# Moving seven buffers of a Fourier-and-attention kernel by 128 bytes, onto multiples of 256

## The chip, the cores and the metric

The kernel runs on one core of a Trainium2 chip. The metric is the device time of one execution in microseconds; the figure given is the median of several runs.

## What is computed

The input x has 2048 rows (the sequence) and 576 columns. A gate mixes linear attention (32 heads of 18 columns) with the real part of a two-dimensional Fourier transform, done as matrix products with given cosine and sine matrices. All data is float32.

```
qkv = x @ wqkv;  phi(t) = where(t > 0, t + 1, exp(t)) + 1e-6
kv  = einsum("bhsd,bhse->bhde", phi(k), v);  z = phi(k) summed over s
o   = einsum("bhqd,bhde->bhqe", phi(q), kv) / (phi(q) . z + 1e-6)
a   = o @ wo
y   = seq_re @ (x @ hid_re.T) - seq_im @ (x @ hid_im.T)
out = g * a + (1 - g) * y,   g = sigmoid((x * gate_w).sum(-1))
```

## The kernel before

**Precision.** Each float32 operand is split into a high part, rounded by ScalarE as it copies (`hi_of`, L175), and a low part, the rest, by VectorE (`lo_of`, L185). A product is three matmuls: high by high, high by low, low by high. Every matmul takes 128 columns of weights (the operand that stays in the array, 512 bytes a partition) and nearly always moves 288 columns past them (half of 576, 1152 bytes a partition). The result goes to one of eight banks.

**Stages, in order.** The K projection (L532, then `run` at L205); the V accumulation, which forms phi(k) times x (L696) and from it the kv matrices (L678, L681); the Q projection (L205, weights `wq`), with the products of kv and wo between; transposes and the output projection (L205, `mw` and `qs`); then, once for the real and once for the imaginary matrices, the hidden transform (L979) and the sequence transform (L1133).

**The two transforms** use a scheme with seven products in place of eight for a two-by-two block matrix: sums and differences of quarters are formed on VectorE (`add`, L195), split into high and low, and multiplied. In `Hidden.run` the order of products is written out by hand: eight passes p over rows of x, in each seven products k, of seven matmuls each (L979), the weights of the array being parts of x (`xf`, `xb`, `xr`) and the moving operand the transform's matrix (`wf`). Its results become the factors `fh` (high) and `fl` (low). In `sequence` 32 batches n follow, each with a piece of the sequence matrix (`craw` as it lands, `c` once split). A batch has seven products of two times three matmuls, 42 in all (L1133): `c` is the weights, `fh` and `fl` the moving operand.

**Buffers.** All tiles lie in one array per partition, the arena, at offsets that are written out by hand. At its start are eight pieces (T_AT) that hold first phi(k) and later the factors, then an accumulator (ACC_AT), then seven slots of 7168 bytes, then small buffers (Y_AT, where the ring `es` of tiles `e` lies, and CONST_AT). Four slots take `craw` and the low parts of `c`, three the high parts; the first batch of each transform lies in the first region, so 62 of the 64 batches are in slots. Between uses the slots hold parts of other stages: tiles of x and the weights `wq` in the K and Q projections, and parts of `xf`, `xb`, `xr` and `wf` in the hidden transforms. The lines that set this:

```
T_AT = 0
ACC_AT = T_AT + NP * TPAIR
SLOT_AT, SLOT = ACC_AT + NT * D * 4 + 256, 7 * BS * P * 4     # L70
Y_AT = SLOT_AT + 7 * SLOT + 512                               # L71
LAY_Q = dict(xs=(-256, 4864, 9984, 43776), hi=(15104, 20864), lo=(26688, 31296))
WF_AT = MIX_AT + 4 * D * 4
WF = 5 * HALF * 4
base = (nc.sbuf_base + 63) // 64 * 64        # every tile lies at base + offset
```

NP is 8, NT 16, D 576, P 128, BS 2, HALF 288, TPAIR 16128 bytes.

`Layout.w(k)` says where the seven `wf` matrices of a hidden transform lie: in the first transform those of k = 3, 4, 5 in slots, in the second those of k = 4, 5, 6, the others beside the accumulator. In the Q projection the four tiles of x lie at the offsets `xs` of LAY_Q (the one at 43776 is replaced by a place in the first region for the Q part), and the weights at `hi` and `lo`, all counted from SLOT_AT.

**What sets the order.** SyncE issues the loads of the sequence matrices (L1070) up to three batches ahead; the orders of TensorE in the later stages, VectorE, ScalarE and SyncE are those in which the program is written. GpSimd issues the stores and loads of the intermediate forms.

Of the kernel before, what the change touches and what calls it, by code (L numbers as in the profile page):

```python
# [14 lines left out]
P = 128  # L15
S, D, H, DH = 2048, 576, 32, 18
NT = S // P
# [8 lines left out]
BS = 2  # L26
# [40 lines left out]
XD = 2 * D * 4  # L67
T_AT = 0
ACC_AT = T_AT + NP * TPAIR
SLOT_AT, SLOT = ACC_AT + NT * D * 4 + 256, 7 * BS * P * 4  # L70
Y_AT = SLOT_AT + 7 * SLOT + 512  # L71
CONST_AT = Y_AT + 2 * D * 4
XS = 10 * P * 4
WH, WL = 5 * HALF * 4, 4 * HALF * 4
# [59 lines left out]
def kernel(  # L134
# [23 lines left out]
    def at(offset, shape, dtype=F, name="t"):  # L158
        count[0] += 1
        t = nc.alloc_sbuf_tensor_at(f"{name}_{count[0]}", list(shape), dtype,  # L160
                                    offset=base + offset)
        return t.ap()
# [200 lines left out]

    es = Ring(Y_AT, 1184, 3)

# [214 lines left out]
    cs_ring = Ring(C_AT, 2 * CU * P * 4, 4)  # L580
    cs_ring.at.append(Y_AT)
    xg_order = [(c, q) for c in range(5) for q in range(NCU)]
# [329 lines left out]
    factors, backlog = [], []  # L912
    y_ring = Ring(Y_AT, HALF * 4, 4)

# [178 lines left out]
    def sequence(m, g, src, dst, last=None, between=None):  # L1093
        late, held, stores, rest_lows = [], [], [], []
        for n in range(NP * NB):
# [45 lines left out]
            if b < NB - 1:  # L1141
                continue
            y = at(Y_AT, [P, 2, 2, HALF], F, "ys")
            c11, c12, c21, c22 = (y[:, i // 2, i % 2] for i in range(4))
# [211 lines left out]
```

## Time and profile before

| | |
|---|---|
| median of 3 runs | 724.93 us (724.75 to 724.96) |
| the profiled execution | 725.31 us, its span 723.6 us |
| TensorE busy | 718.9 us, 5436 matmuls |
| VectorE, ScalarE, GpSimd busy | 594.6, 331.8, 54.1 us |
| moved by DMA | 157.83 MB, mean 218 GB/s |
| granted TensorE clock | 1.000 |

The profile is of one execution. Busy time of an engine is the union of its instructions; matmuls overlap one another, since each is recorded from its start to its modelled end (about 294 ns), while the next starts some 130 ns after it. What a matmul costs is thus the distance from its start to the next one's, not its recorded length.

### The profile page before, as it was taken

To read this page: it belongs to the slowest core of one execution; us is meant where nothing else is said; L and a number is where in the kernel's file an instruction comes from. 1 tells how busy PE (TensorE), PEld (TensorE's weight loads), DVE (VectorE), ACT (ScalarE), POOL (GpSimd) and SP (SyncE) were. 2 spreads that over 40 slices of the span, in tenths; PEclk is the share of its full clock that TensorE was granted. 3 is DMA by queue.
4 is the path that set the end of the run, shared out by engine and by line. 5 is a ranking of instruction groups with operands and counts; after the bars stand their busy time and mean duration, and the time that the engine had idled before them with its cause. 6 is when DMAs were issued, how large, how long until landed. Compare 5 with 4: busy or idle time off the path is not lost.

```text
span 723.6 us, 13786 instructions
## 1 busy us (share of the span) xinstructions
PE 718.9 (99%) x5436; PEld 718.3 (99%) x5436; DVE 594.6 (82%) x954; ACT 331.8 (46%) x519; POOL 54.1 (7%) x94
## 2 busy tenths in 40 slices
PE   9999999999999999999999999999999999999998
PEld 9999999999999999999999999999999999999997
DVE  5699876787999828989999999857889988778884
ACT  5998445678644534453434334223535432342331
POOL 1112200050131100000010000000000000000000
PEclk9999999999999999999999999999999999999999
DMA  7388887874594699544475586889963543454440
GB/s 256 105 286 297 305 304 214 295 223 118 182 358 177 228 321 388 160 153 131 157 249 189 167 289 198 287 313 401 380 214 130 175 143 136 125 179 153 153 154 34
DMA packets 54836, 157.83 MB, mean 218 GB/s; under 512 B 6388, under 2 KB 12084, under 8 KB 53748
## 3 DMA queue, kind: packets, MB, share of 16 engines
q1 hardware_dynamic: 45716, 118.44, 48.5%
q0 software_dynamic: 8768, 38.12, 14.5%
q8 instruction: 43, 0.70, 0.4%
q10 hardware_dynamic: 288, 0.39, 0.2%
q14 instruction: 21, 0.17, 0.1%
HBM read 114.06 MB, written 41.39 MB: 215 GB/s over the span
## 4 chain that ended last, share of the span: by engine, by line
PE 93%; DVE 6%; issue 0%; ACT 0%; DVEq 0%; POOL 0%; POOLq 0%
PE bank L1133 49%; PE bank L205 18%; PE bank L979 14%; PE bank L696 8%; PE bank L532 2%; DVE qs L185 1%; DVE acc L775 1%; DVE pz L767 1%; DVE den L768 1%; PE bank L231 1%; PE bank L678 0%; DVE xb L185 0%; DVE den L772 0%; PE bank L797 0%; DVE xb L195 0%
## 5 line engine op out<-in xcount | busy, mean ns | idle before, releaser
L1133 PE MATMUL bank<-fh,c 128*128 128x288 f32 x1792 | 354.7, 294 | 0.0
L1133 PEld LDWEIGHTS bank<-fh,c 128*128 128x128 f32 x1792 | 286.7, 188 | 0.0
L1133 PE MATMUL bank<-fl,c 128*128 128x288 f32 x896 | 263.6, 294 | 0.0
L175 ACT ACTIVATE c<-craw 128x1792 fp32r<-128x1792 f32 (+1 forms) x84 | 121.3, 1447 | 169.9 <-DVE craw L195 161.2
L1133 PEld LDWEIGHTS bank<-fl,c 128*128 128x128 f32 x896 | 168.7, 188 | 0.0
L185 DVE TENSOR_TENSOR c<-craw,c 128x1792 fp32r<-128x1792 f32 (+4 forms) x86 | 141.9, 1653 | 1.5 <-ACT c L175 1.4
L195 DVE TENSOR_TENSOR craw<-craw 128x256 f32<-128x256 f32 (+1 forms) x192 | 97.9, 512 | 22.0 <-DMA craw<-in_ci_dram 13.6
L205 PE MATMUL bank<-wd,xs 128*128 128x288 f32 (+1 forms) x784 | 105.9, 295 | 0.0
L205 PEld LDWEIGHTS bank<-wd,xs 128*128 128x128 f32 x784 | 104.6, 188 | 0.0
L979 PE MATMUL bank<-wf,xf 128*128 128x288 f32 x588 | 91.1, 295 | 0.0
L979 PEld LDWEIGHTS bank<-wf,xf 128*128 128x128 f32 x588 | 83.4, 189 | 0.0
L205 PE MATMUL bank<-mw,qs 128*128 128x288 f32 x448 | 61.8, 296 | 0.1
L696 PE MATMUL bank<-pk,c 128*128 128x288 f32 x448 | 60.6, 296 | 0.0
L205 PEld LDWEIGHTS bank<-mw,qs 128*128 128x128 f32 x448 | 59.8, 188 | 0.5 <-DVE qs L185 0.4
L696 PEld LDWEIGHTS bank<-pk,c 128*128 128x128 f32 x448 | 59.7, 189 | 0.0
L370 DVE SCALAR_TENSOR_TENSOR acc<-bank,e 128x288 f32<-128x288 f32 x64 | 28.5, 452 | 17.3 <-ACT e L369 17.1
L195 DVE TENSOR_TENSOR ys<-bank,ys 128x288 f32<-128x288 f32 x63 | 28.8, 456 | 16.0 <-PE bank L1133 12.6
L185 DVE TENSOR_TENSOR fl<-fl,fh 128x864 fp32r<-128x864 f32 (+1 forms) x32 | 34.5, 1093 | 6.6 <-ACT fh L175 5.3
L175 ACT ACTIVATE fh<-fl 128x864 fp32r<-128x864 f32 (+1 forms) x32 | 29.8, 950 | 16.6 <-DVE fl L195 16.6
L195 DVE TENSOR_TENSOR fl<-bank,y 128x288 f32<-128x288 f32 x48 | 21.6, 450 | 15.8 <-PE bank L979 15.8
L979 PE MATMUL bank<-wf,xr 96*128 96x288 f32 x112 | 33.3, 298 | 0.0
L195 DVE TENSOR_TENSOR ys<-ys,bank 128x288 f32<-128x288 f32 x47 | 21.2, 450 | 12.4 <-PE bank L1133 11.8
(106 smaller groups left out, 639.6 us busy)
## 6 DMA issues: line engine op xcount, KB each, us to landing
xf<-xm SPq DMA_DIRECT2D x42, 512.0 KB, 8.4
craw<-in_cr_dram SPq DMA_DIRECT2D x32, 512.0 KB, 3.6
craw<-in_ci_dram SPq DMA_DIRECT2D x32, 512.0 KB, 3.7
xm<-xb POOLq DMA_DIRECT2D x8, 1024.0 KB, 5.8
wf<-wm SPq DMA_DIRECT2D x14, 576.0 KB, 6.2
xraw<-in_xa_dram SPq DMA_DIRECT2D x25, 320.0 KB, 3.5
xr<-xr SPq DMA_DIRECT2D x14, 448.0 KB, 8.0
xm<-xb POOLq DMA_DIRECT2D x8, 768.0 KB, 7.4
```

Of the source, the lines that this page charges most:

```text
L175: return nc.scalar.activation(dst, src, AF.Copy, bias=bias)
L185: nc.vector.tensor_tensor(out=dst, in0=src, in1=hi, op=ALU.subtract)
L195: nc.vector.tensor_tensor(out=dst, in0=a, in1=b, op=op)
L205: nc.tensor.matmul(ps, a, b, start=(n == 0), stop=(n == len(pairs) - 1))
L231: nc.tensor.matmul(warm[:, :P], ones_f, ones_f, start=True, stop=True)
L370: nc.vector.scalar_tensor_tensor(dst, ps, 0.0, e, op0=ALU.max, op1=ALU.add)
L532: nc.tensor.matmul(ps[i][h], x[:, i_x * P:(i_x + 1) * P], wkt.row(h, j), start=(c == 0 and n == 0), stop=(c == KC and n == 1))
L696: nc.tensor.matmul(ps[h][:, :HALF], t[:, a, k], pk[s][:, b, half(h)], start=(s == 0 and n == 0), stop=(s == NT - 1 and n == len(passes) - 1))
L767: nc.vector.scalar_tensor_tensor(pz, acc[2 * k + i], EPS, zb, op0=ALU.add, op1=ALU.mult)
L768: nc.vector.tensor_reduce(out=d[:, i], in_=pz.rearrange("p (h d) -> p h d", d=DH), op=ALU.add, axis=AX.X)
L979: nc.tensor.matmul(ps, a, b, start=(start and n == 0), stop=(n == len(ops) - 1), skip_group_check=True)
L1133: nc.tensor.matmul(ps[q], c[x][:, l, k], factors[p](y, f), start=(p == 0 and i == 0), stop=(p == NP - 1 and i == 2))
```

## The change

The start of the slots moves up by 128 bytes, and the gap behind the slots shrinks by as much, so that Y_AT and all behind it stay. In the built program the arena's base is at byte 1152, which is 128 past a multiple of 256; the slots began 128 past such a multiple and begin on one now. No instruction is added, removed or moved on any engine; 289 tiles change their address by 128 bytes: the `c` and `craw` in slots (186 of them), and `xf`, `xs`, `xraw`, `xb`, `wf`, `wd`, `wraw`, `xr`, three tiles of wo and one constant for the warm-up.

```diff
-SLOT_AT, SLOT = ACC_AT + NT * D * 4 + 256, 7 * BS * P * 4
-Y_AT = SLOT_AT + 7 * SLOT + 512
+SLOT_AT, SLOT = ACC_AT + NT * D * 4 + 384, 7 * BS * P * 4
+Y_AT = SLOT_AT + 7 * SLOT + 384
```

## The prediction

> **What bounds the kernel now.** I read the page's engine line first, then who waited for whom on TensorE, then the chain of work that ended last, and last the timeline of single products.
>
> ```profile
> PE 718.9 (99%) x5436; PEld 718.3 (99%) x5436; DVE 594.6 (82%) x954; ACT 331.8 (46%) x519; POOL 54.1 (7%) x94
> ...
> PE bank L231 <- POOL ones_f L224: 1.1, 1, 1.1
> PEld bank L205 <- DVE qs L185: 0.4, 1, 0.4
> ```
>
> The first row is the page: TensorE is busy for 718.9 of 723.6 us. The other two are all the waits that TensorE has in the whole run, with its weight loads: 1.1 us for the first memset and 0.4 us once in the output projection. No transfer is waited for by TensorE anywhere. So the time is a count of matmuls multiplied by the distance between their starts (the pace), and the chain shows the pace by stage:
>
> ```profile
> 20.42 44.59 PE bank L205 x336
> 65.01 19.18 PE bank L696 x144
> 85.16 12.85 PE bank L696 x96
> ...
> 261.68 51.98 PE bank L979 x392
> 313.66 177.16 PE bank L1133 x1344
> 490.82 52.07 PE bank L979 x392
> 542.89 174.03 PE bank L1133 x1320
> ```
>
> Columns: start, length, line, number of matmuls. Length over number gives 132.7 ns for the K projection (L205), 133.2 and 133.9 for the V accumulation (L696), 132.6 and 132.8 for the hidden products (L979), and 131.8 in both sequence stages (L1133). All are 288 columns wide, with weights of 128 columns, at the same granted clock:
>
> ```profile
> 262.00:314.00 52.00, 52.00 (x394) 52.00 (x393) 41.10 (x80) 22.25 (x39) 1.86 (x3) 1.00 0.75 266
> 314.00:491.00 177.00, 177.00 (x1345) 177.00 (x1344) 155.44 (x214) 63.94 (x46) 6.42 (x9) 1.00 0.65 220
> 491.00:543.00 52.00, 52.00 (x394) 52.00 (x392) 42.93 (x83) 21.78 (x38) 0.00 (x0) 1.00 0.89 330
> ```
>
> The last three numbers of a row are granted clock, DMA share and GB/s. The clock is 1.00 in all three stages, and the DMA share goes from 0.65 to 0.89 with the pace moving by 1 ns: the pace does not follow the transfers. What is left to explain 131.8 against 133.9 is the order of the operands and where they lie. That is all this change touches.
>
> **What the addresses are.** In the built program the arena starts at byte 1152 of a partition, 128 past a multiple of 256. T_AT, ACC_AT, the old SLOT_AT and a slot's size are multiples of 256 within it, and weights of 128 columns are 512 bytes. So every full set of weights that lies in a slot now starts 128 past a multiple of 256, and will start on one. Moving operands are 1152 bytes, 4.5 times 256, so neighbours alternate between the two places. No instruction, tile size, buffer reuse or wait changes.
>
> **Part by part.** The sum is made against the profiled execution's own 725.31 us (span 723.6, 1.71 around it); the median of the three runs, 724.93, is 0.38 below it.
>
> *Sequence products (L1133).* 62 of the 64 batches lie in slots, so 62 x 42 = 2604 matmuls get weights that start 128 bytes higher; their moving factors stay. No row shows this stage with weights on a multiple of 256. The nearest row is the stage itself: its batches go round through different slots in the two runs, and both come to 131.8. Whether the weight load could be the limit is seen in the kv-by-wo products before the output projection:
>
> ```profile
> 145.04 1.75 PE L205 MATMUL bank<-plain,kvb 126*126 126x288 f32 x12
> 146.64 3.89 PE L205 MATMUL bank<-wd,xs 128*128 128x288 f32 x28
> 150.37 1.74 PE L205 MATMUL bank<-plain,kvb 126*126 126x288 f32 x12
> 151.94 3.90 PE L205 MATMUL bank<-wd,xs 128*128 128x288 f32 x28
> 155.68 0.95 PE L205 MATMUL bank<-plain,kvb 72*72 72x288 f32 x6
> 156.47 0.70 PE L205 MATMUL bank<-wd,xs 128*128 128x288 f32 x4
> ```
>
> Start to start, the 126-column weights run at 1.60/12 = 133 and 1.57/12 = 131 ns; they begin at all sorts of offsets, since a row of kvb is 126 wide. The 72-column weights, little more than half as much to load, run at 0.79/6 = 132. A load that is almost halved and one at any offset make no pace of their own. I take 0 for this part. The bounds: the fastest six in the next fence run at 130.0 ns, 1.8 below, which is -4.7 us for 2604; L696's slowest row, 133.9, is 2.1 above, +5.5 us.
>
> *Hidden products (L979).* Three of the seven weight matrices of each run lie in slots, and here they are the moving operand; they shift against the other four.
>
> ```profile
> 262.45 0.96 PE L979 MATMUL bank<-wf,xb 128*128 128x288 f32 x6
> 263.25 0.30 PE L979 MATMUL bank<-wf,xr 96*128 96x288 f32 x1
> 263.38 0.95 PE L979 MATMUL bank<-wf,xb 128*128 128x288 f32 x6
> 264.17 0.30 PE L979 MATMUL bank<-wf,xr 96*128 96x288 f32 x1
> 264.31 0.95 PE L979 MATMUL bank<-wf,xb 128*128 128x288 f32 x6
> 265.09 0.30 PE L979 MATMUL bank<-wf,xr 96*128 96x288 f32 x1
> 265.23 0.96 PE L979 MATMUL bank<-wf,xb 128*128 128x288 f32 x6
> 266.03 0.30 PE L979 MATMUL bank<-wf,xr 96*128 96x288 f32 x1
> 266.17 0.95 PE L979 MATMUL bank<-wf,xb 128*128 128x288 f32 x6
> ```
>
> These are products k = 1 to 4 and the start of k = 5. A product is seven matmuls. Their blocks of weights are 5760 bytes, 22.5 times 256, so the high parts start on a multiple of 256 for k = 1 and 4 and 128 past one for k = 2 and 3. From start to start the products take 0.93 and 0.94 us on the multiple, 0.93 and 0.92 off it: 0.01 us more on it, which is as small as the rows can show. (The six of k = 3 take 265.09 - 264.31 = 0.78, 130.0 each.) In the first run two blocks go onto a multiple and one leaves it, in the second all three go onto one: four products more per pass, eight passes, 32 x 0.01 = **+0.3 us**. Bounds 0 and, if each rounding goes against it, +0.6.
>
> By the Trainium skill (SBUF — State Buffer, Who interferes with whom) TensorE reads moving operand and weights through two ports of its own and never waits for another engine; taken strictly, both parts would be 0 and the two rivals on pace below would fall. The rows agree as to the other engines, and differ a little on places, by 0.01 us a product, so I keep those rivals.
>
> *Projections.* In the K projection 336 matmuls get moved weights under unmoved moving operands; the row is 132.7 ns, and the output is as for L1133: 0. In the Q projection all 448 moving operands shift, but half of the chunks lie on a multiple and half off it, and they change places: the two rows of 28 above run at 3.73/28 = 133.2 and 3.74/28 = 133.6. 0; bounds +-0.6 us by the same 0.01 us per seven.
>
> *VectorE and ScalarE.* They split and sum the slots. Where one operation is seen at several places its time stays:
>
> ```profile
> L369 ACT ACTIVATE e<-e x64: 443/445/447, 19.0 to 195.7; 128x288 f32<-128x288 f32 x64
> L370 DVE SCALAR_TENSOR_TENSOR acc<-bank,e x64: 444/451/459, 19.5 to 198.2; 128x288 f32<-128x288 f32 x64
> ```
>
> The ring of e has three places 1184 bytes apart, 128, 32 and 192 past a multiple of 256. Least, median and most lie within 4 ns and 15 ns. Cost 0, hidden under TensorE; without that cover, 8 ns for each of some 192 sums would be 1.5 us.
>
> *Transfers into slots.* Of the loads that move, the sequence matrices are the ones somebody waits for:
>
> ```profile
> craw<-in_cr_dram SPq DMA_DIRECT2D x32, 512.0 KB, 3.6
> craw<-in_ci_dram SPq DMA_DIRECT2D x32, 512.0 KB, 3.7
> ...
> DVE craw L195 <- DMA craw<-in_ci_dram: 13.6, 10, 2.8
> DVE craw L195 <- DMA craw<-in_cr_dram: 4.0, 5, 1.7
> ```
>
> VectorE waits 17.6 us for them in all, TensorE none: it eats the batch made before. I take 0; the bound is 1.5 us, all of TensorE's waits.
>
> The sum: 725.31 + 0.3 = 725.6, less 0.38 to the median: **725.2 us**.
>
> **Rivals.** 0.2% of the median, about what a measurement of this kernel can tell from no change, is 1.45 us; spread over 2604 matmuls that is 0.55 ns of pace.
>
> *Slower: the sequence pace is a lucky one.* 131.8 is the lowest of all stages; the same matmul runs at 132.6 to 133.9 where the operands stand to each other in another way. If moving the weights alone takes L1133 to the K projection's 132.7, it costs 0.9 x 2604 = 2.3 us: 727.5. At L696's 133.9 it is 730.7. For it: the stage is half of the time, and it is the only one whose two operands shift against each other throughout. Against it: the 72- and 126-column rows. It decides from 0.55 ns a matmul.
>
> *Faster: weights on the boundary let the next matmul start sooner.* At 130.0 ns, the fastest six of the trace, -4.7 us: 720.5; half of that 722.9. For it: such a pace exists. Against it: it is found with weights off the boundary.
>
> *Faster: the loads.* Loads that start on a multiple land sooner, and VectorE's 17.6 us shrink. TensorE has only 1.5 us of waits, so 723.7 at best, and none of them on a load. By the Trainium skill (DMA: Bandwidth & Descriptors, How a descriptor splits into AXI transactions) a piece that starts off a 256-byte boundary fetches from the boundary below; a row of 4096 bytes would be 16 transactions in place of 17, which I estimate at 3% of beats. No run here shows that yet.
>
> *It does not do what it says*: excluded, since the arena's start puts the slots on the boundary.
>
> **How the numbers follow.** Forecast (within 1.45 us) 0.42; slower by pace 0.35; faster by pace 0.20; by the loads 0.03. Slower gets more than faster since the stage already has the best pace, and any other is likelier worse. Predicted 725.2. The range takes most of both pace rivals and leaves out their far ends: from 721.5 (3.7 of the 4.7 us that 130.0 ns would bring) to 729.0 (133.2 ns, L696's better row, is 1.4 ns above 131.8: +3.6 us, 728.8).
>
> **What would show it.** The chain's two L1133 rows should stay at 177.2 and 174.0 us; each 0.1 ns of pace is 0.13 us there. Above 178.2 the slower rival is right, below 176.1 the faster. The L979 rows should gain about 0.1 and 0.2 us, with k = 3 and 4 changing places. VectorE's 17.6 us of waiting tells on the loads; if it halves and the time stays, they were hidden. A new wait of TensorE on any engine would make the whole reading wrong.

## The result, and the profile after

The changed kernel takes 727.58 us in the median of five runs, the one before 724.75 us beside it: 2.83 us longer, a ratio of 1.004 with a 95% interval of 1.0028 to 1.0051. The page of the changed kernel's profiled execution (728.72 us, span 727.0):

```profile
span 727.0 us, 13786 instructions
...
PE 722.3 (99%) x5436; PEld 721.7 (99%) x5436; DVE 595.0 (82%) x954; ACT 331.3 (46%) x519; POOL 54.0 (7%) x94
```

All waits of TensorE and of its weight loads (total us, times, longest):

```profile
PE bank L231 <- POOL ones_f L224: 1.1, 1, 1.1
...
PEld bank L205 <- DVE qs L185: 0.3, 1, 0.3
```

TensorE is busy 3.4 us longer with the same 5436 matmuls, and still waits for nobody. The chain that ended last (start, length, line, number) says where:

```profile
20.82 44.52 PE bank L205 x336
65.33 18.72 PE bank L696 x144
...
261.61 52.11 PE bank L979 x392
313.72 178.88 PE bank L1133 x1344
492.60 52.17 PE bank L979 x392
544.77 175.58 PE bank L1133 x1320
```

The two sequence runs grew by 1.72 and 1.55 us, from 131.8 to 133.1 and 133.0 ns a matmul; the hidden ones by 0.13 and 0.10. That is 3.5 us, and the span grew by 3.4.

The hidden transform starts at 261.61 us, as before (261.68), but two things cancel there. The first row begins 0.40 us later; where it begins differs from run to run (19.5 to 20.9 us in the nine whole kernels traced for this study). And the first 144 matmuls of the V accumulation (L696) take 18.72 us in place of 19.18, which is 130.0 ns each in place of 133.2, although none of their operands has moved. This row has 18.72 us in each of the three among these nine whose slots are moved by 128 bytes against the rest, and 19.18 to 19.20 in the other six.

(The median moved by less, since the execution that was profiled is 1.1 us above the median of its kernel and that of before 0.6 above its own.)

The loads (KB each, median us to landing), and VectorE's waits for them:

```profile
craw<-in_cr_dram SPq DMA_DIRECT2D x32, 512.0 KB, 3.6
craw<-in_ci_dram SPq DMA_DIRECT2D x32, 512.0 KB, 3.7
```

```profile
DVE craw L195 <- DMA craw<-in_ci_dram: 12.7, 11, 2.2
...
DVE craw L195 <- DMA craw<-in_cr_dram: 7.1, 5, 3.5
```

The loads land after 3.6 and 3.7 us, as before, and VectorE waits 19.8 us for them, not less than 17.6. Starting on a multiple of 256 did nothing for them that can be seen.

### The profile page after: what moved, and what is told of

The parts are those of the page before. It is cut to its first block, busy times and chain, and to the rows that moved or that the text cites. A ratio compares the mean times of both kernels' runs of the same rounds, so it can differ in the third digit from the quotient of the medians.

```text
span 727.0 us, 13786 instructions
## 1 busy us (share of the span) xinstructions
PE 722.3 (99%) x5436; PEld 721.7 (99%) x5436; DVE 595.0 (82%) x954; ACT 331.3 (46%) x519; POOL 54.0 (7%) x94
## 4 chain that ended last, share of the span: by engine, by line
PE 93%; DVE 6%; issue 0%; ACT 0%; DVEq 0%; POOL 0%; POOLq 0%
PE bank L1133 49%; PE bank L205 18%; PE bank L979 14%; PE bank L696 8%; PE bank L532 2%; DVE qs L185 1%; DVE acc L775 1%; DVE pz L767 1%; DVE den L768 1%; PE bank L231 1%; PE bank L678 0%; DVE xb L185 0%; DVE den L772 0%; PE bank L797 0%; DVE xb L195 0%
## 5 line engine op out<-in xcount | busy, mean ns | idle before, releaser
L1133 PE MATMUL bank<-fh,c 128*128 128x288 f32 x1792 | 357.9, 295 | 0.0
L1133 PEld LDWEIGHTS bank<-fh,c 128*128 128x128 f32 x1792 | 287.4, 188 | 0.1
L1133 PE MATMUL bank<-fl,c 128*128 128x288 f32 x896 | 263.9, 295 | 0.0
L1133 PEld LDWEIGHTS bank<-fl,c 128*128 128x128 f32 x896 | 168.7, 188 | 0.0
L696 PE MATMUL bank<-pk,c 128*128 128x288 f32 x448 | 60.1, 295 | 0.0
L696 PEld LDWEIGHTS bank<-pk,c 128*128 128x128 f32 x448 | 59.3, 188 | 0.0
```

The source lines that it names most:

```text
L696: nc.tensor.matmul(ps[h][:, :HALF], t[:, a, k], pk[s][:, b, half(h)], start=(s == 0 and n == 0), stop=(s == NT - 1 and n == len(passes) - 1))
L1133: nc.tensor.matmul(ps[q], c[x][:, l, k], factors[p](y, f), start=(p == 0 and i == 0), stop=(p == NP - 1 and i == 2))
```

## The experiments

### Is it where the weights lie, or how they lie to the moving operand?

Three kernels. The first is the one before with the whole arena 128 bytes higher, the second the changed one with the same, the third has the slots up by 256.

```diff
 all_up_128 (of before), change_and_all_up_128 (of the changed kernel)
-    base = (nc.sbuf_base + 63) // 64 * 64
+    base = (nc.sbuf_base + 63) // 64 * 64 + 128
 slots_up_256 (of before)
-SLOT_AT, SLOT = ACC_AT + NT * D * 4 + 256, 7 * BS * P * 4
-Y_AT = SLOT_AT + 7 * SLOT + 512
+SLOT_AT, SLOT = ACC_AT + NT * D * 4 + 512, 7 * BS * P * 4
+Y_AT = SLOT_AT + 7 * SLOT + 256
```

> The kernel before with its whole arena 128 bytes higher: weights in slots and moving factors both shift, and stand to each other as before. Relative theory (the pace of a sequence product follows from where weights lie against the moving operand, modulo 256): as before, 724.8 us and 131.8 ns a matmul in both sequences. Absolute theory (weights of 512 bytes that start on a multiple of 256 are slower to load): as after the change, 727.6 us and 133.0 ns. Rival on transfers (loads that start on a multiple of 256 disturb something): 727.6 too, since the loads into slots are on multiples here.

> The changed kernel with its whole arena 128 bytes higher: weights in slots are back at 128 past a multiple of 256, the moving factors are now the ones that shifted. Relative theory: as after the change, 727.6 us and 133.0 ns. Absolute theory: as before, 724.8 us and 131.8 ns.

> Slots 256 bytes higher than before, all else as before. If 256 is the period: 724.8 us and 131.8 ns by the relative and the absolute theory alike. If the period is 512 or more (a bank or a row of the memory): another pace than 131.8, up to the 133.0 of the changed kernel or beyond.

Measured against the kernel before on the same chip (725.1 us): 725.18 us, 1.0002 (0.9993 to 1.0012); 728.17 us, 1.0042 (1.0027 to 1.0057); 725.34 us, 1.0003 (0.9994 to 1.0012). The sequence runs in the chain of the first two, and the second run of the third (in its first, the execution that was profiled, 727.1 us long, has TensorE waiting 1.2 us for VectorE's `c`, so that run is no measure of the pace):

```profile
313.52 177.16 PE bank L1133 x1344
...
542.76 174.03 PE bank L1133 x1320
```

```profile
312.60 178.75 PE bank L1133 x1344
...
543.53 175.58 PE bank L1133 x1320
```

```profile
544.71 174.03 PE bank L1133 x1320
```

With everything moved, the weights on multiples of 256 run at the old pace to the hundredth; with the weights back at their old place modulo 256 but the factors moved, they run at the new one. So neither the weights' own place nor that of the loads counts: it is how weights and moving operand lie to each other, and a shift by 256 bytes changes nothing.

### TensorE alone

The sequence stage's order of matmuls, on zeros, with nothing beside it: each case is eight batches of 42 with its own line. The three numbers of a case are the shifts, in bytes, of the factors, the high and the low parts of the weights.

```
case(0, 0, 0, ...)         # L71, L89      case(0, 0, 128, ...)     # L76
case(0, 128, 128, ...)     # L72           case(0, 64, 64, ...)     # L77
case(128, 0, 0, ...)       # L73           case(0, 32, 32, ...)     # L79
case(128, 128, 128, ...)   # L74           case(0, 256, 256, ...)   # L80
case(0, 128, 0, ...)       # L75           case(0, 512, 512, ...)   # L81
```

> TensorE alone: the sequence stage's order of matmuls on zeros, eight batches a case, with no VectorE, ScalarE or DMA work beside it; the rest of the computation is left out. Cases shift factors, high parts and low parts of the weights by bytes. If the pace is TensorE's own matter: 131.7 ns for the layout before (first and last case), 133.0 with both weights up 128. Rival (other engines' or the DMAs' accesses to the slots slow TensorE): 131.7 in both. Factors up 128 alone: 133.0 by the relative theory, 131.7 by the absolute one; all three up 128: 131.7 and 133.0. Only high or only low parts up: each theory leaves it open, some value between. Shifts of 32, 64, 192: by either theory like one of the two, if only the number of 256-byte blocks counts.

The chain of this run:

```profile
97.92 44.66 PE bank L72 x336
142.58 44.68 PE bank L73 x336
187.26 44.27 PE bank L74 x336
231.52 44.57 PE bank L75 x336
276.10 44.59 PE bank L76 x336
320.68 44.51 PE bank L77 x336
...
409.76 44.74 PE bank L79 x336
454.50 44.27 PE bank L80 x336
498.76 44.27 PE bank L81 x336
...
854.62 44.29 PE bank L89 x336
```

Length over 336 (L71, the first case, holds the start and is not used): the old layout 131.8 ns (L89), the new one 132.9 (L72), factors moved alone 133.0 (L73), all moved 131.8 (L74), by 256 and by 512 131.8. TensorE does all of this by itself; the rival on other engines and transfers falls. Moving only the high or only the low parts gives 132.6 and 132.7, about three quarters of the whole. 32 bytes are worse than 128 (133.2), 64 lie between (132.5), so counting 256-byte blocks does not explain it.

### The same shifts in the whole kernel

```diff
 slots_up_32 (of before; slots_up_64 in the same way, with 320 and 448)
-SLOT_AT, SLOT = ACC_AT + NT * D * 4 + 256, 7 * BS * P * 4
-Y_AT = SLOT_AT + 7 * SLOT + 512
+SLOT_AT, SLOT = ACC_AT + NT * D * 4 + 288, 7 * BS * P * 4
+Y_AT = SLOT_AT + 7 * SLOT + 480
```

> Slots 32 bytes higher than before. TensorE alone ran this at 133.2 ns against 131.8: 1.4 x 2604 = 3.7 us, 728.5, worse than the change itself. Theory that only the number of 256-byte blocks touched counts: as before, 724.8.

> Slots 64 bytes higher than before. TensorE alone ran this at 132.4 to 132.5 ns: 0.7 x 2604 = 1.8 us, 726.6, between before and the change. Theory that only the number of 256-byte blocks touched counts: as before, 724.8.

Measured, with 725.25 us for the kernel before: 729.32 us, 1.0057 (1.0043 to 1.0071), and 727.07 us, 1.0027 (1.0016 to 1.0039). The sequence runs of the first in the chain, then the first run of the second:

```profile
314.50 178.92 PE bank L1133 x1344
...
545.57 175.74 PE bank L1133 x1320
```

```profile
313.07 178.07 PE bank L1133 x1344
```

Both runs of the first come to 133.1 ns and the second to 132.5, as TensorE alone had it to 0.1 ns. 64 bytes cost less than the change itself, as expected: this first run is 0.8 us shorter than the changed kernel's. That 32 cost more is less sure: the two sequence runs are 0.2 us longer than the changed kernel's, the V accumulation lacks the 0.46 us gained there, and the intervals of the totals overlap.

### Single pairs

> TensorE alone again, on zeros, the rest of the computation left out. First single pairs, 168 times the same matmul: moving operand at 0 or 128, weights at 0 to 224 past a multiple of 256. If each pair has a pace of its own that follows from the distance of the two operands modulo 256, the eight distances differ among one another (by some ns, as 131.8 and 133.0 do), and moving operand 128 with weights 128 equals 0 with 0. Rival: what counts is the jump from one matmul's operands to the next's; then all pairs that repeat are alike, and only those that alternate between two places differ. Then the sequence stage's order with other orders of its three matmuls, other gaps and pitches of the factors. By the first theory a pitch of 1280 bytes (all factors at the same place modulo 256) gives one clean pace, the best or worst of the pairs; by the rival it gives the best, since nothing jumps.

One matmul repeated 168 times with fixed operands, and a few cases of the sequence's order. In the chain:

```profile
69.09 22.12 PE bank L79 x168
91.21 22.40 PE bank L80 x168
...
158.41 22.41 PE bank L83 x168
180.81 22.12 PE bank L84 x168
202.93 22.21 PE bank L85 x168
...
247.54 22.40 PE bank L87 x168
...
292.16 22.12 PE bank L89 x168
...
336.68 22.38 PE bank L91 x168
359.06 22.38 PE bank L92 x168
...
448.07 22.26 PE bank L96 x168
...
514.68 44.32 PE bank L98 x336
...
603.79 44.25 PE bank L100 x336
...
826.31 44.11 PE bank L105 x336
...
1048.12 44.24 PE bank L110 x336
1092.36 44.80 PE bank L111 x336
```

L79 to L86 have the weights 0, 32, 64 ... 224 bytes past the moving operand, modulo 256: a distance of 0 (L79) and of 160 (L84) runs at 131.7 ns, 192 (L85) at 132.2, the others at 133.3 to 133.4 (shown for 32 and 128). Moving the moving operand by 128 gives 133.3 with the weights left (L87) and 131.7 with the weights moved too (L89): the distance again. So a pair has a pace of its own, from 131.7 to 133.4, as the first theory says. L110 and L111 say the same for the sequence: with a pitch of 1280 bytes all its factors have one distance to the weights, and it runs at 131.7 ns with 0 and at 133.3 with 128, where the rival has the best pace for both.

But a mix need not be the mean of its pairs. L91 and L92 alternate the moving operand, between distances of 0 and 128, and run at 133.2, not 132.5; L96 alternates the weights between the same distances and does run at 132.5.

The sequence stage is such a mix. Its weights all start at one place modulo 256, its factors, 1152 bytes apart, at two. Counted from the program, before the change 22 of a batch's 42 matmuls have distance 0 and 20 have 128; after it, 20 and 22. By the paces of the pairs alone the change would cost 0.1 ns a matmul; it cost 1.2. So it is not that the pairs got slower ones on the whole: the order in which the distances follow one another must count too.

L98 and L100 are the sequence with its first two matmuls exchanged, on old and new slots: 131.9 and 131.7. L105, the lowest of all cases, has the high parts alone 64 bytes up and the order high by high, low by high, high by low: 131.3; in the whole kernel the slots adjoin, so the high parts can't move alone, and it was not run there. L98 and L100 pointed to the next two kernels.

### Undoing the loss without moving a byte

```diff
 change_other_order (of the changed kernel), before_other_order (of before)
-                        for i, (x, y) in enumerate(TURN if n or b else FULL):
+                        for i, (x, y) in enumerate(FULL):
```

TURN is high by low, high by high, low by high; FULL has the first two exchanged.

> The changed kernel, slots 128 bytes higher, with the three matmuls of a sequence product in the order high by high, high by low, low by high in all batches (the first two exchanged against before). Relative theory with the order in it: TensorE alone ran this at 0.3 ns a matmul below the layout before, so the 2.8 us are gone with the addresses still moved: 724.3 us, each sequence run as before or up to 0.4 us shorter. Rival (moved slots cost by themselves, through loads, VectorE or the weights' own address): 727.6.

> The kernel before with that other order of the three matmuls, as a control. Relative theory with the order: TensorE alone showed no difference here, 724.8 us. Rival (the other order is better of itself, by a later or earlier need of the low factors): 724.0 or less.

Measured, with 725.25 us for the kernel before: 724.71 us, 0.9993 (0.9985 to 1.0002), and 727.98 us, 1.0037 (1.0024 to 1.0051). The sequence runs of the first, then the second:

```profile
312.46 176.90 PE bank L1133 x1344
...
541.53 173.84 PE bank L1133 x1320
```

```profile
313.74 178.57 PE bank L1133 x1344
...
544.37 175.38 PE bank L1133 x1320
```

On the moved slots the other order takes the whole loss away: 131.6 and 131.7 ns, 0.26 and 0.19 us below before in the two runs. The total is no worse than before, and its interval does not quite exclude 1; it has the lowest median of this study, but is not shown to beat the one before. No operand has moved against the changed kernel and every pair is the same: only the order differs. The control failed its expectation: the old slots in the other order run at 132.9 ns in the kernel, though TensorE alone had 131.9. The same addresses in the same order have two paces.

### Two paces for one layout

> TensorE alone, on zeros, the rest of the computation left out. Four layouts (old and new slots, each in the old and the other order of the three matmuls), eight batches each, started several times behind different stretches of 37 to 50 matmuls of one repeated pair. If the pace carries a state from one matmul to the next, the old slots in the other order settle at 131.8 ns behind some beginnings and at 132.9 behind others (132.9 is what the whole kernel showed, 131.8 what TensorE alone did), and perhaps other layouts too have two settled paces. If the addresses alone decide, each layout has the same pace behind every beginning, and the 132.9 in the whole kernel comes from something else in it.

Each case stands behind some 40 matmuls of one pair; the odd lines between are those. In the chain:

```profile
74.96 44.67 PE bank L80 x336
...
125.22 44.32 PE bank L82 x336
...
175.27 44.27 PE bank L84 x336
...
324.32 44.67 PE bank L90 x336
...
425.36 44.30 PE bank L94 x336
...
676.34 44.69 PE bank L104 x336
...
929.11 44.22 PE bank L114 x336
```

L80 to L92 are old slots in the other order: 132.9 ns behind a pair at distance 0 (L80) or 192 (L90), 131.9 and 131.8 behind the five others (128 and 64 shown, L82 and L84). Addresses and order of the case itself are the same. The banks of the results differ from case to case, but they also change within a case, at its fifth batch, and both paces last through that. So the pace carries a state from one matmul to the next, and this layout can settle in two. The beginnings differ in their pair and in their number of matmuls (37 to 50); which of the two decides was not separated. The other three had one settled pace each behind all of five beginnings (one of each shown): old slots and old order 131.8 (L94), new slots and old order 133.0 (L104), new slots and other order 131.6 (L114). What that state is stays open.

The V accumulation may be a case of it in the whole kernel: its own addresses stay, the K projection just ahead of it has its weights moved, and its first 144 matmuls run at 130.0 ns in place of 133.2. No run tests that by itself.

## Why the prediction was right or wrong

*What bounds the kernel*: right. TensorE's count times pace, no wait, and nearly all of the time came with the pace of L1133.

*The forecast of no change* (725.2 us, chance 0.42) was wrong. The measured 727.58 is the slower rival, with a chance of 0.35, and lies in the range.

*The term that failed* is the first, the sequence products at 0: they cost 1.72 + 1.55 = 3.3 us in the profiled execution, 1.2 ns a matmul, inside the bounds of -4.7 and +5.5. The argument for 0 was that weights of 72 and 126 columns at any offset make no pace of their own. That the weights' own place makes none is true, as all_up_128 shows, but it was the wrong question: those rows mix many distances to the moving operand, and tell nothing of one run of distances in one order. The same holds for "the batches go round through different slots": slots lie multiples of 256 apart, so every batch had the same run of distances. What the runs show in place of the 0 is 133.0 ns for 131.8, by TensorE alone, whenever the weights move by 128 against the factors in this order of the matmuls.

*What the sum left out* is the V accumulation: as none of its operands moves, it has no term, and its first row fell by 0.46 us.

*The slower rival* gave the mechanism (the operands stand to each other in another way) and the place, and its sign came: the first L1133 row reads 178.88 us, above 178.2. It took the K projection's 132.7 ns, +2.3 us, 727.5; the pace became 133.0. That 727.5 is so near 727.58 is partly luck: 2.3 us upon 725.2, where the medians differ by 2.83 from 724.75. It said that the stage already has the best pace and any other is likelier worse; the single pairs bear that out, as 131.7 is the lowest of eight distances and five of the eight run at 133.3 or more. It also called the stage the only one whose operands shift against each other throughout. Those of the K projection do too, by the prediction's own account, and cost nothing (44.59 and 44.52 us): a shift of 128 bytes does not always cost.

*The faster rival on pace*: wrong for the sequence, whose order of matmuls came under 131.3 in no layout that was tried (L105 among the single pairs' cases). The 130.0 ns that it took from six matmuls does exist as a lasting pace: the V accumulation has it for 144 matmuls after the change.

*Hidden products, +0.3*: 0.13 + 0.10 measured, about that size, with a wrong reason: the place modulo 256 does not count, since all_up_128 moves everything and has 51.98 and 52.07 us as before. In the first pass `xb` lies in a slot as well, so k = 3 and 4 kept their distances and did not change places as foretold (0.92 and 0.93 us after, 0.92 and 0.94 before).

*Projections, VectorE, ScalarE*: 0 each was right within 0.1 us (K projection 44.59 and 44.52, VectorE 594.6 and 595.0 us busy).

*Loads*: 0 was right, and so was the small chance of the rival. The Trainium skill's rule on descriptors (DMA: Bandwidth & Descriptors, How a descriptor splits into AXI transactions) gave an estimate of 3% here; the landing times of 3.6 and 3.7 us did not move. Only the side in SBUF was moved, so no run shows the rule for the side that is read.

*The Trainium skill's rule of the two ports* (SBUF — State Buffer, Who interferes with whom), taken strictly, would have made the change free. That other engines do not slow TensorE's matmuls agrees with the runs: the sequence has 131.8 and 133.0 ns in the kernel and alone. That its two operands cannot matter to each other does not: 131.7 against 133.4 ns for one pair, by distance alone.

## What to carry to other kernels

In a stage where TensorE never waits, look at the distance of weights and moving operand modulo 256 and at the order in which the distances follow, not at either's alignment: a tidy address cost 0.9% of this stage. A few hundred matmuls on zeros show the pace of a layout, and an order of the matmuls inside a product may give back what a layout takes. When a row is to show that something does not matter, see first whether it holds fixed what the change will move.

## What was not expected of the hardware

Matmuls of 288 float32 columns that never wait are not of one length: single pairs settle at 131.7, 132.2 or about 133.3 ns by their distance modulo 256, and mixes run at 130.0 (the V accumulation after the change) to 133.9 (its later rows before). For one layout and order, two settled paces, 131.8 and 132.9 ns, were reached from different beginnings. Each lasted to the end of its case of eight batches, and the slower one, in the whole kernel, through both sequence runs.
